# Expert slots of 512 tokens instead of 256, and the last batch finished inside the first slot

## The chip, the cores and the metric

The kernel runs on one core of one Trainium2 chip. The metric is the device time of one execution in microseconds (us). One execution of the kernel before was also taken with the hardware profiler; all rows below are of that execution, and times in them count from the start of its span.

## The reference

What is computed is hashed attention followed by a mixture of experts with one expert per token (all float32):

```
q, k, v: (4, 8, 768, 64)          proj: (64, 6)
bucket(z) = the 6 signs of z @ proj, read as a number
attn = softmax over keys in the query's bucket of 0.125 * q @ k^T   # else -1e9
x    = attn @ v, heads side by side            # (3072, 512)
logits = x @ w_gate + modality_bias[modality_id]      # 8 experts
e = argmax(logits);  g = softmax(logits)[e]
out[token] = g * (relu(x[token] @ w1[e]) @ w2[e])     # w1 512x1024, w2 1024x512
```

With the reference's inputs four of the eight experts get tokens: 1477, 1469, 98 and 28 of the 3072.

## The kernel before

There are two stages. The attention stage works on 16 pairs of heads (4 batches of 4 pairs; pair 15 is the last). Its TensorE order is written out by hand: the strings PLAN, one for each of six key steps (kt 0 to 5) of a pair, say in which order scores (S, lines 305 and 306), the weighted sums of values (A, line 341), the maxima of the next pair (M), the next pairs' preparation (T, B) and the finishing of an earlier batch follow each other. The softmax sums of a pair are added up by GpSimd, and for pair 15 half of them by VectorE (line 326, tile sp); sums(i), line 354, turns them into one row for each query with TensorE (line 361). finish(b), line 368, makes a batch's gate logits (lines 376 to 413) and calls route, line 593, which chooses the experts and scatters token numbers and gate weights into the table tab in DRAM (line 635). finish_x(b), line 417, turns a batch's x by TensorE (line 424), scales it on VectorE (line 426, tile xs, two buffers) and stores it to x_d in DRAM (line 428; from SyncE's queue, for the last batch from ScalarE's), in six tiles. Batch 2's six tiles are done in pairs 14 and 15, by the letters x and y of PLAN: in pair 15 tiles 3, 4 and 5 in the steps kt 2, 4 and 5. sums(15) is the last piece of the attention stage (line 518).

The expert stage (line 723) works in slots. A slot holds 256 tokens of one expert (TS, line 526; nt is 2) or, a small slot, 128. For a slot the token numbers come from tab by SyncE's queue (line 770), x is gathered by GpSimd's indirect DMA, 128 tokens at a time (line 774, tile xg), turned by TensorE (line 785) and split into a high and a low part by ScalarE and VectorE (lines 786 and 787, tiles xh and xl). The 4 MB of an expert's weights come in eight tiles of 512 KB (lines 752 and 754, tile raw, 4 buffers), and each is split in two parts (line 760 on ScalarE, line 762 on VectorE, for some of the first on GpSimd; tile w, 7 buffers). Tiles 0 to 3 of a slot are the first product (gemm1, line 790): two groups of 12 matmuls (lines 797 to 799) for each, whose result hps (PSUM, 3 buffers) is read by ScalarE (line 803) and then VectorE (line 804). Tiles 4 to 7 are the second product (gemm2, line 832, lines 839 to 841) into yps (PSUM, one bank per 128 tokens); store (line 843) scales by the gate weight and scatters to out (lines 846 and 847). Small slots go by gemm1_small and turn_small.

Each expert's tokens go to as many 256-slots as its count needs (a remainder up to 128 goes to a small slot). Two slots are early: they hold tokens of batches 0 to 2 alone, so that they don't wait for batch 3. After them come 10 sure slots and 2 sure small ones; further slots stand in conditional blocks behind them. In body (line 937) the order before is: the early slots' table (early_slots, line 685), x of the first slot, the first weights, all of finish(3), the tables of the late slots (late_slots, line 697), then slot 0 interleaved with finish_x(3), and the other slots. The slots in order are two early, eight late, a small one, two late, a small one.

In the expert stage the order on each engine is made by a scheduler from priorities in the order of the program and its own picture of time; every engine then runs its list in order. SBUF of the expert stage is that of the attention stage's tiles, given out from the bottom in the order of the pools.

Of the kernel before, what the change touches and what calls it, by code (L numbers as in the profile page):

```python
# [74 lines left out]
def attention(ctx, actx, tc, a, x_d, l_d, route=None, setup=None):  # L75
# [341 lines left out]
    def finish_x(b, lo, hi):  # L417
# [29 lines left out]
    with tc.manual_schedule(engines={mybir.EngineType.PE}):  # L447
# [19 lines left out]
        for i in range(NPR):  # L467
# [9 lines left out]
            for kt in range(NT):  # L477
                for c in PLAN[kt]:
# [39 lines left out]
        sums(NPR - 1)  # L518
# [7 lines left out]
TS = 256  # L526
DUMMY = E * N
EARLY = CFG["early"]
NBIG, SURE_BIG = 13, 12 - EARLY
NSML, SURE_SML = 8, 2  # L530


def host_consts_moe():
    def rep(x):
# [5 lines left out]
        "c_step": rep(np.stack([np.arange(12) * 256.0 + 255.5, np.arange(12) * 256.0 + 128.5])),  # L540
# [5 lines left out]
def router(ctx, tc, a, x_d, tab):  # L546
# [5 lines left out]
    step = const.tile([P, 2, 12], F32, name="kstep")  # L552
# [91 lines left out]
    def above(cnt, row, name):  # L644
        g = wk.tile([P, E, 12], F32, name="sg")
        nc.vector.tensor_tensor(out=g, in0=cnt.unsqueeze(2).broadcast_to([P, E, 12]), in1=step[:, row].unsqueeze(1).broadcast_to([P, E, 12]), op=ALU.is_gt)
# [76 lines left out]
def experts(ctx, tc, a, x_d, tab, out, ps_x, ident):  # L723
    nc = tc.nc
    w1, w2 = a["moe_w1"], a["moe_w2"]
    xp = ctx.enter_context(tc.tile_pool(name="xp", bufs=2))
    raw = ctx.enter_context(tc.tile_pool(name="raw", bufs=CFG["raw"]))
# [3 lines left out]
    hp = ctx.enter_context(tc.tile_pool(name="hp", bufs=10))  # L731
    ps_h = ctx.enter_context(tc.tile_pool(name="eps_h", bufs=3, space=PSUM))
    ps_y = ctx.enter_context(tc.tile_pool(name="eps_y", bufs=3, space=PSUM))
# [4 lines left out]

    def nt(s):
        return 1 if s[0] == "s" else 2  # L740
# [16 lines left out]
    def split(r, n):  # L757
        w = (wa if n % CFG["wp"] < 3 else wb).tile([P, 2, 1024], F32R, name="w")
        hi, lo = w[:, 0], w[:, 1]
        nc.scalar.copy(out=hi, in_=r)  # L760
        pool = n % 2 == 1 if n < CFG["pn"] else n % 8 in CFG["pm"]
        (nc.gpsimd if pool else nc.vector).tensor_tensor(out=lo, in0=r, in1=hi.bitcast(F32), op=ALU.subtract)  # L762
        return hi, lo

    def gather(s):
# [3 lines left out]
        tb = xp.tile([P, 2, 2], I32, name="tb", bufs=CFG["fd"] + 2)  # L769
        nc.sync.dma_start(out=tb[:, 0:n], in_=tab[bass.ds(o, n * P), :].rearrange("(p a) w -> p a w", a=n))  # L770
        xg = xp.tile([P, 2, DM], F32, name="xg", bufs=CFG["fd"] + 1)
        src = x_d[0:(B - 1) * S] if s[0] == "e" else x_d
        for g in range(n):
            nc.gpsimd.indirect_dma_start(out=xg[:, g], out_offset=None, in_=src, in_offset=bass.IndirectOffsetOnAxis(ap=tb[:, g, 0:1], axis=0))  # L774
        return tb, xg

    def xprep(s, xg):
        n = nt(s)
        xh = xp.tile([P, 4, TS], F32R, name="xh")
        xl = xp.tile([P, 4, TS], F32R, name="xl")  # L780
        for c in range(0, 4, 2):
            tp = ps_x.tile([P, 2, TS], F32, name="psx")
            for cc in range(2):
                for g in range(n):
                    nc.tensor.transpose(tp[:, cc, g * P:(g + 1) * P], xg[:, g, (c + cc) * P:(c + cc + 1) * P], ident)
            nc.scalar.copy(out=xh[:, c:c + 2, 0:n * P], in_=tp[:, :, 0:n * P])
            nc.vector.tensor_tensor(out=xl[:, c:c + 2, 0:n * P], in0=tp[:, :, 0:n * P], in1=xh[:, c:c + 2, 0:n * P].bitcast(F32), op=ALU.subtract)
        return xh, xl

    def gemm1(hi, lo, xh, xl, hh, hl):  # L790
        hi = hi.rearrange("p (c f) -> p c f", c=4)
        lo = lo.rearrange("p (c f) -> p c f", c=4)
        for fb in range(2):
# [8 lines left out]
            with tc.high_priority(offset=CFG["hpo"]):  # L802
                nc.scalar.activation(th, hps, AF.Relu)  # L803
                nc.vector.scalar_tensor_tensor(out=tl, in0=hps, scalar=0.0, in1=th.bitcast(F32), op0=ALU.max, op1=ALU.subtract)  # L804
# [3 lines left out]
    def gemm1_small(hi, lo, xh, xl):  # L808
        hi = hi.rearrange("p (c f) -> p c f", c=4)
        lo = lo.rearrange("p (c f) -> p c f", c=4)  # L810
        hps = ps_h.tile([P, TS], F32, name="hps")
# [4 lines left out]
        h = hp.tile([P, TS], F32, name="hn", bufs=2)  # L816
# [3 lines left out]
    def turn_small(h, hh, hl):  # L820
        tp = ps_h.tile([P, TS], F32, name="hps")
# [4 lines left out]
        nc.scalar.copy(out=th, in_=tp)  # L826
        nc.vector.tensor_tensor(out=tl, in0=tp, in1=th.bitcast(F32), op=ALU.subtract)  # L827
# [22 lines left out]
    class Runner:  # L850


        def __init__(self):
            self.raws, self.ws, self.got, self.xs = {}, {}, {}, {}
# [7 lines left out]
        def ahead(self):  # L862
            LS, LL = CFG["LS"], CFG["LL"]
            while True:
                did = False
                if self.nl < min(len(self.seq), self.n + LL + 1) and self.nl - self.ns < CFG["raw"]:
# [3 lines left out]
                elif self.ns < min(self.nl, self.n + LS + 1):  # L870
# [10 lines left out]
        def prepare(self, s):  # L881
            self.fetch(s)
            if s not in self.xs:
                self.xs[s] = xprep(s, self.got[s][1])

        def slot(self, k):
# [4 lines left out]
            for j in range(8):  # L891
                self.ahead()
                if j == CFG["fj"] and k > 0:
                    for s2 in self.order[k + 1:k + 1 + CFG["fd"]]:
                        self.fetch(s2)
                if j == 4:
                    yps = [ps_y.tile([P, DM], F32, name="yps") for _ in range(nt(s))]
                    if nxt:
                        self.prepare(nxt)
# [6 lines left out]
                elif nt(s) == 2:  # L906
# [27 lines left out]
    return Runner, tabs, conditional  # L934


def body(tc, a, out):
# [3 lines left out]
    with ExitStack() as ctx, ExitStack() as actx:  # L941
# [3 lines left out]
        runner, tabs, conditional = experts(ctx, tc, a, x_d, tab, out, ps_x, ident)  # L945
# [42 lines left out]
```

## Time and profile before

| | us |
|---|---|
| median of 3 runs | 866.99 |
| lowest, highest | 864.04, 867.5 |
| the profiled execution | 862.96 |
| its span | 861.1 |
| TensorE busy in the span | 801.3 |
| VectorE, ScalarE, GpSimd busy | 600.8, 498.3, 457.2 |
| mean granted TensorE clock | 0.977 of full speed |

The profiled execution lasted 862.96 us, of which 861.1 us are the span that the rows cover. Engines are PE (TensorE; PEld its weight loads), DVE (VectorE), ACT (ScalarE), POOL (GpSimd) and SP (SyncE, whose DMA queue is SPq). An arrow out<-in names the tile that is written and those that are read; xN is a count. A bracket at the end of a row gives the idle time of the engine before it and what ended that. Matmuls overlap in the pipeline, so that the time from one start to the next, and not a row's own length, is what one costs.

### The profile page before, as it was taken

How to read it: one execution, taken by the hardware profiler on the slowest of the kernel's cores; microseconds unless marked ns; L12 is line 12 of the kernel's file. 1: busy time of each engine (PE TensorE's matmuls, PEld its weight loads, DVE VectorE, ACT ScalarE, POOL GpSimd, SP SyncE). 2: the span in 40 equal slices, each digit the busy share in tenths (PEclk: the TensorE clock that was granted, in tenths of full speed). 3: DMA queues.
4: the chain of work that ended last, by engine and by line, in shares of the span. 5: the costliest groups of instructions: out<-in, count | busy, mean ns of one | idle time of the engine just before them, and what ended most of it. 6: DMA issues, size and time to landing. Idle time of an engine off the chain costs nothing.

```text
span 861.1 us, 14524 instructions
## 1 busy us (share of the span) xinstructions
PE 801.3 (93%) x5154; PEld 590.9 (69%) x5154; DVE 600.8 (70%) x1029; ACT 498.3 (58%) x953; POOL 457.2 (53%) x347
## 2 busy tenths in 40 slices
PE   6799999999999999999989787889999999999993
PEld 3466666666667656566746345779999999998992
DVE  6777678797877897776877767766555565567650
ACT  4567676676667566566744343355555555557551
POOL 5377779677887867976667664232222221122110
PEclk9899999999999999999999797999999999999997
DMA  6423212320431132132101254597777767679650
GB/s 173 112 75 92 74 43 68 93 74 19 118 116 63 55 93 74 56 99 68 38 19 31 72 160 147 113 325 222 222 218 232 222 214 234 200 230 299 215 148 22
DMA packets 76753, 110.87 MB, mean 129 GB/s; under 512 B 10495, under 2 KB 52095, under 8 KB 76672
## 3 DMA queue, kind: packets, MB, share of 16 engines
q1 hardware_dynamic: 70880, 95.14, 37.4%
q0 software_dynamic: 4928, 13.14, 4.1%
q10 hardware_dynamic: 864, 1.57, 0.6%
q8 instruction: 43, 0.70, 0.3%
q14 instruction: 38, 0.31, 0.2%
HBM read 84.83 MB, written 13.33 MB: 114 GB/s over the span
## 4 chain that ended last, share of the span: by engine, by line
PE 75%; DVE 10%; issue 6%; DMA 4%; ACT 2%; POOL 1%; SPq 1%; POOLq 0%; DVEq 0%; ACTq 0%
PE psu L341 13%; PE pss L305 8%; PE pss L306 7%; PE psm L239 5%; PE yps L839 5%; PE yps L841 5%; PE yps L840 5%; PE hps L797 4%; PE hps L799 4%; PE hps L798 4%; PE psx L207 3%; PE psx L180 3%; PE psm L245 3%; PE psx L222 2%; PE psx L268 1%
## 5 line engine op out<-in xcount | busy, mean ns | idle before, releaser
L326 POOL TENSOR_TENSOR sp<-sp,pb 128x768 f32<-128x768 f32 x124 | 224.9, 1849 | 38.3 <-ACT pb L323 38.1
L762 DVE TENSOR_TENSOR w<-raw,w 128x1024 fp32r<-128x1024 f32 x108 | 138.9, 1287 | 99.6 <-ACT w L760 93.7
L241 DVE TENSOR_REDUCE mx<-psm 128x1 f32<-128x512 f32 x192 | 131.3, 687 | 41.6 <-PE psm L239 40.4
L760 ACT CAST w<-raw 128x1024 fp32r<-128x1024 f32 x112 | 116.9, 1047 | 69.7 <-PE yps L841 50.7
L341 PE MATMUL psu<-pb,vt 128*64 128x512 f32 (+1 forms) x768 | 137.4, 501 | 0.0
L318 ACT ACTIVATE pb<-pss 128x512 f32<-128x512 f32 x192 | 112.9, 609 | 27.1 <-PE pss L306 18.6
L797 PE MATMUL hps<-xh,w 128*128 128x256 f32 x384 | 109.4, 286 | 2.1 <-DVE hl L804 1.9
L798 PE MATMUL hps<-xl,w 128*128 128x256 f32 x384 | 109.1, 284 | 0.0
L799 PE MATMUL hps<-xh,w 128*128 128x256 f32 x384 | 108.8, 284 | 0.0
L341 PEld LDWEIGHTS psu<-pb,vt 128*64 128x64 f32 x768 | 51.8, 139 | 79.8 <-issue 73.1
L774 POOL DMA_INDIRECT xg<-x_d,tb x26 | 32.7, 1259 | 123.6 <-DMA tb<-tab 115.7
L847 POOL DMA_INDIRECT out<-y,tb x26 | 33.9, 1305 | 117.2 <-ACT y L846 63.9
L839 PE MATMUL yps<-w,hl 128*128 128x512 f32 x208 | 82.9, 398 | 0.9 <-DVE hl L827 0.9
L841 PE MATMUL yps<-w,hh 128*128 128x512 f32 x208 | 81.3, 391 | 0.0
L840 PE MATMUL yps<-w,hh 128*128 128x512 f32 x208 | 81.0, 389 | 0.0
L323 ACT ACTIVATE pb<-pss 128x512 f32<-128x512 f32 x96 | 57.7, 601 | 38.5 <-PE pss L306 36.0
L305 PE MATMUL pss<-m_0g,s_0g 128*128 128x512 f32 x192 | 71.5, 372 | 6.3 <-DVE m_0g L270 3.9
L797 PEld LDWEIGHTS hps<-xh,w 128*128 128x128 f32 x384 | 73.9, 193 | 3.5 <-DVE hl L804 2.6
L798 PEld LDWEIGHTS hps<-xl,w 128*128 128x128 f32 x384 | 73.9, 192 | 1.2 <-issue 0.8
L799 PEld LDWEIGHTS hps<-xh,w 128*128 128x128 f32 x384 | 73.8, 192 | 0.0
L803 ACT ACTIVATE hh<-hps 128x256 fp32r<-128x256 f32 x96 | 36.6, 384 | 64.0 <-PE hps L799 57.9
L305 PE MATMUL pss<-m_1g,s_1g 128*128 128x512 f32 x192 | 69.5, 362 | 1.2 <-ACT pb L323 0.8
(214 smaller groups left out, 1773.3 us busy)
## 6 DMA issues: line engine op xcount, KB each, us to landing
raw<-moe_w SPq DMA_DIRECT2D x112, 512.0 KB
qk<-q SPq DMA_DIRECT2D x32, 192.0 KB
qk<-k SPq DMA_DIRECT2D x32, 192.0 KB
vt<-v SPq DMA_DIRECT2D x16, 384.0 KB
x_d<-xs SPq DMA_DIRECT2D x18, 256.0 KB
m_1g<-m_1g SPq DMA_DIRECT2D x16, 192.0 KB
s_1g<-s_1g SPq DMA_DIRECT2D x16, 192.0 KB
m_0g<-m_0g SPq DMA_DIRECT2D x15, 192.0 KB
```

The lines of the kernel that those rows point to most:

```text
L241: nc.vector.tensor_reduce(out=mx[:, qt + j, hi, 0:1], in_=mp, axis=AX.X, op=ALU.max)
L305: nc.tensor.matmul(out, t["s1"][h][:, ks], t["m1"][h][:, cs], start=True, stop=False)
L326: (nc.vector if h and i in CFG["spd"] else nc.gpsimd).tensor_tensor(out=t["sp"][:, h], in0=(t["pb"][0] if kt == 1 else t["sp"])[:, h], in1 ...
L341: nc.tensor.matmul(t["u"][part][64 * h:64 * h + 64, 0:w], t["v"][:, h, kt], t["pb"][kt][:, h, COLS[part]], start=False, stop=(kt == NT - 1 ...
L760: nc.scalar.copy(out=hi, in_=r)
L762: (nc.gpsimd if pool else nc.vector).tensor_tensor(out=lo, in0=r, in1=hi.bitcast(F32), op=ALU.subtract)
L797: nc.tensor.matmul(hps, lo[:, c, fs], xh[:, c], start=(c == 0), stop=False)
L798: nc.tensor.matmul(hps, hi[:, c, fs], xl[:, c], start=False, stop=False)
L799: nc.tensor.matmul(hps, hi[:, c, fs], xh[:, c], start=False, stop=(c == 3))
L839: nc.tensor.matmul(yps[g], hl[fc][:, gs], hi[:, fb], start=(fc == 0), stop=False)
L840: nc.tensor.matmul(yps[g], hh[fc][:, gs], lo[:, fb], start=False, stop=False)
L841: nc.tensor.matmul(yps[g], hh[fc][:, gs], hi[:, fb], start=False, stop=(fc == 7))
```

## The change

Slots hold 512 tokens (TS = 512): two early, four sure and two small ones, 8 slots in place of 14. gemm1's matmuls are 512 columns wide instead of 256, xprep turns four groups of tokens and is cut into halves that are done in the last two steps of the slot before. The pools change: two xg buffers of 512 tokens, one xh and xl, 5 buffers of w instead of 7, two of hps instead of three, four of yps instead of three, 8 of hh and hl. For early slots the token numbers are first limited to those of batches 0 to 2 by an operation on GpSimd (tile at). sums(15) moves from the end of the attention stage to the start of finish(3). All of finish(3) and finish_x(3) are interleaved with the eight steps of slot 0; the x tiles of batch 3 use the four buffers of y. In pair 15 tiles 3, 4 and 5 of batch 2's x are done ahead of the first score of kt 0, 1 and 2. late_slots and the late slots' tables follow slot 0.

```
@@ finish
+        if 4 * b + 4 == NPR:
+            sums(NPR - 1)
+            yield
@@ finish_x
-            xs = bp.tile([P, 512], F32, name="xs", bufs=2)
+            xs = pool.tile([P, 512], F32, name="y") if pool else bp.tile([P, 512], F32, name="xs", bufs=2)
@@ attention, the loop over pairs
             for kt in range(NT):
+                if i == NPR - 1 and kt < 3:
+                    next(xs, None)
+                    next(xs, None)
...
-        sums(NPR - 1)
@@ sizes
-TS = 256
+TS = 512
-NBIG, SURE_BIG = 13, 12 - EARLY
+NBIG, SURE_BIG = 11, 6 - EARLY
+RAW, WP, XG, LL = 4, 5, 2, 8
@@ experts
-    xp = ctx.enter_context(tc.tile_pool(name="xp", bufs=2))
+    gp = ctx.enter_context(tc.tile_pool(name="gp", bufs=1))
-    wa = ctx.enter_context(tc.tile_pool(name="wa", bufs=3))
-    wb = ctx.enter_context(tc.tile_pool(name="wb", bufs=CFG["wp"] - 3))
+    xp = ctx.enter_context(tc.tile_pool(name="xp", bufs=1))
+    wp = ctx.enter_context(tc.tile_pool(name="wp", bufs=WP))
+    hp = ctx.enter_context(tc.tile_pool(name="hp", bufs=8))
-    ps_h = ctx.enter_context(tc.tile_pool(name="eps_h", bufs=3, space=PSUM))
-    ps_y = ctx.enter_context(tc.tile_pool(name="eps_y", bufs=3, space=PSUM))
+    ps_h = ctx.enter_context(tc.tile_pool(name="eps_h", bufs=2, space=PSUM))
+    ps_y = ctx.enter_context(tc.tile_pool(name="eps_y", bufs=4, space=PSUM))
@@ gather
+            at = gp.tile([P, TS // P, 1], I32, name="at", bufs=2)
+            nc.gpsimd.tensor_scalar(out=at, in0=tb[:, :, 0:1], scalar1=(B - 1) * S - 1, scalar2=None, op0=ALU.min)
@@ slot
-                if j == CFG["fj"] and k > 0:
-                    for s2 in self.order[k + 1:k + 1 + CFG["fd"]]:
+                if j in (1, 4):
+                    for s2 in self.order[k + 1:k + 2 + j // 4]:
                         self.fetch(s2)
                 if j == 4:
                     yps = [ps_y.tile([P, DM], F32, name="yps") for _ in range(nt(s))]
-                    if nxt:
-                        self.prepare(nxt)
+                if j in (6, 7) and nxt:
+                    self.prepare(nxt, False)
@@ body
-            for _ in finish(B - 1):
-                pass
+        drive([(r.slot(0), 8, 0, 1), (chain(finish(B - 1), finish_x(B - 1, 0, NT, yp)), 26, 0.02, 1)])
         tabs["b"], tabs["s"], tot = late_slots()
...
-            drive([(r.slot(0), 8, 0, 1), (finish_x(B - 1, 0, NT), 12, 0, CFG["fxe"])])
```

## Rows read from the trace of the kernel before

**Rows 1.** The page's first part: busy time, share of the span and instructions of each engine.

```profile
PE 801.3 (93%) x5154; PEld 590.9 (69%) x5154; DVE 600.8 (70%) x1029; ACT 498.3 (58%) x953; POOL 457.2 (53%) x347
```

**Rows 2.** Stretches of time: the stretch in us from the span's start, its length, then busy us and instructions of PE, PEld, DVE, ACT and POOL, the granted PE clock, the DMA engines' busy share and GB/s. The first is the end of pair 14 and the start of pair 15, then the change from attention to experts, then about one full slot, and the end.

```profile
480.00:500.00 20.00, 13.71 (x64) 7.70 (x60) 12.38 (x10) 8.36 (x16) 9.66 (x6) 0.82 0.46 143
...
520.00:545.00 25.00, 19.40 (x144) 15.96 (x145) 21.59 (x50) 7.78 (x15) 10.96 (x8) 0.80 0.52 172
...
599.00:622.00 23.00, 23.00 (x152) 21.11 (x152) 13.74 (x19) 12.95 (x20) 5.37 (x4) 1.00 0.74 227
...
840.00:861.00 21.00, 7.36 (x40) 5.99 (x39) 1.27 (x3) 2.17 (x6) 1.19 (x2) 0.79 0.07 23
```

**Rows 3.** The same view over the whole expert stage up to its last matmul.

```profile
516.60:847.40 330.80, 317.94 (x2065) 285.68 (x2061) 206.88 (x318) 178.46 (x278) 78.75 (x60) 0.98 0.68 212
```

**Rows 4.** The chain that ended last, in two neighbouring full slots (start, us, what): the turns of x in one slot and in the next; the first and last of the 48 matmuls of a second product; the first and the last but one shown of a first product (84 matmuls from the one to the other, 83 steps).

```profile
599.93 0.87 PE psx L785 x8
623.23 0.87 PE psx L785 x8
...
624.10 0.23 PE yps L839
...
634.80 0.23 PE yps L841
635.03 0.12 PE hps L797
...
644.98 0.12 PE hps L799
```

**Rows 5.** The last small slot and the end of TensorE's work (the view of instructions in order of time: start, us, engine, line, operation): its first and its last matmul, then the last scatter.

```profile
835.04 0.28 PE L813 MATMUL hps<-w,xh 128*128 128x256 f32 x1
...
846.97 0.39 PE L841 MATMUL yps<-w,hh 128*128 128x512 f32 x1
...
848.36 0.98 POOL L847 DMA_INDIRECT out<-y,tb  x1 [8.15 <-ACT y L846]
```

**Rows 6.** Groups of instructions by line and form from 576 to 834 us: count, busy us, mean ns of one, and the idle time before them: the splitting of weights by VectorE and ScalarE, and the operations of both that read 512 columns out of PSUM.

```profile
L762 DVE TENSOR_TENSOR w<-raw,w 128x1024 fp32r<-128x1024 f32 x92 | 112.7, 1225 | 89.0 <-ACT w L760 87.5 <-PE hps L799 0.7 <-issue 0.5
L760 ACT CAST w<-raw 128x1024 fp32r<-128x1024 f32 x92 | 96.3, 1047 | 55.1 <-PE yps L841 49.9 <-DMA raw<-moe_w 3.1 <-issue 2.2
...
L787 DVE TENSOR_TENSOR xl<-psx,xh 128x512 fp32r<-128x512 f32 x20 | 12.8, 681 | 0.0
...
L786 ACT CAST xh<-psx 128x512 fp32r<-128x512 f32 x20 | 10.8, 595 | 0.5 <-PE psx L785 0.5
```

**Rows 7.** TensorE from the end of attention into the first slot, in order of time.

```profile
514.13 2.80 PE L341 MATMUL psu<-pb,vt 128*64 128x512 f32 x16
516.86 1.26 PE L361 MATMUL psx<-sp,ones 128*32 128x384 f32 x8
521.30 0.66 PE L785 MATMUL psx<-ident,xg 128*128 128x128 f32 x2 [3.19 <-DMA xg<-x_d,tb]
...
527.59 2.79 PE L376 MATMUL psx<-ut,gst 128*32 128x512 f32 x16 [2.38 <-DVE xl L787]
530.31 0.58 PE L798 MATMUL hps<-xl,w 128*128 128x256 f32 x1
```

**Rows 8.** The same view of the other engines there: the last three stores of batch 2's x on SyncE's queue, GpSimd's last addition of sums, its first gather for the first slot and its splitting of weights, and VectorE's splitting of weights.

```profile
504.45 10.82 SPq L428 DMA_DIRECT2D x_d<-xs  x3
...
514.60 1.82 POOL L326 TENSOR_TENSOR sp<-sp,pb 128x768 f32<-128x768 f32 x1 [1.81 <-ACT pb L323]
517.77 0.99 POOL L774 DMA_INDIRECT xg<-x_d,tb  x1 [1.35 <-DMA x_d<-xs]
...
520.04 4.67 POOL L762 TENSOR_TENSOR w<-raw,w 128x1024 fp32r<-128x1024 f32 x2
...
519.41 7.53 DVE L762 TENSOR_TENSOR w<-raw,w 128x1024 fp32r<-128x1024 f32 x2 [0.68 <-ACT w L760]
```

**Rows 9.** Pair 15's first steps on TensorE, in order of time: tile 2 of batch 2's x, the last of the four score matmuls that ran in kt 0 before the stall, the first behind it, the values' sums of kt 1, and the first score of kt 2.

```profile
481.64 0.63 PE L424 MATMUL psx<-ident,ut 128*128 128x128 f32 x4
...
483.83 0.40 PE L306 MATMUL pss<-m_1g,s_1g 128*128 128x512 f32 x1
488.10 0.55 PE L305 MATMUL pss<-m_0g,s_0g 128*128 128x256 f32 x1 [3.88 <-DVE m_0g L270]
...
490.57 4.40 PE L341 MATMUL psu<-pb,vt 128*64 128x512 f32 x16
...
498.22 0.50 PE L305 MATMUL pss<-m_0g,s_0g 128*128 128x512 f32 x1 [2.13 <-ACT pb L318]
```

**Rows 10.** VectorE and GpSimd over the same time: an operation on two elements a partition, for the early slots' table, the reader of a PSUM tile behind it, the scaling of tile 2, and GpSimd's additions of sums.

```profile
479.10 8.34 DVE L682 TENSOR_SCALAR selr<-selr 128x2 f32<-128x2 f32 x1
...
488.45 0.42 DVE L271 TENSOR_SCALAR lone<-psx 128x256 fp32r<-128x256 f32 x1
488.90 0.69 DVE L426 TENSOR_TENSOR xs<-psx,rin 128x512 f32<-128x512 f32 x1
...
473.22 14.19 POOL L326 TENSOR_TENSOR sp<-sp,pb 128x768 f32<-128x768 f32 x8
```

**Rows 11.** Whom TensorE waited for from 516 to 848 us: total us, times, the longest.

```profile
PE psx L785 <- DMA xg<-x_d,tb: 4.8, 4, 3.2
PE psx L376 <- DVE xl L787: 2.4, 1, 2.4
```

More of the change, by code (lines that the diff above doesn't have):

```diff
@@ L644, in above @@
     def above(cnt, row, name):
-        g = wk.tile([P, E, 12], F32, name="sg")
-        nc.vector.tensor_tensor(out=g, in0=cnt.unsqueeze(2).broadcast_to([P, E, 12]), in1=step[:, row].unsqueeze(1).broadcast_to([P, E, 12]), op=ALU.is_gt)
+        g = wk.tile([P, E, NSTEP], F32, name="sg")
+        nc.vector.tensor_tensor(out=g, in0=cnt.unsqueeze(2).broadcast_to([P, E, NSTEP]), in1=step[:, row].unsqueeze(1).broadcast_to([P, E, NSTEP]), op=ALU.is_gt)
         nb = wk.tile([P, E], F32, name=name)
@@ L775, in gather, with xprep @@
         return tb, xg
-    def xprep(s, xg):
-        n = nt(s)
+    def xprep(s, xg, dst):
         xh = xp.tile([P, 4, TS], F32R, name="xh")
         xl = xp.tile([P, 4, TS], F32R, name="xl")
[L781 to L788, printed above, removed]
+        dst += [xh, xl]
+        if nt(s) == 1:
+            tp = ps_x.tile([P, 4, P], F32, name="psx")
+            for c in range(4):
+                nc.tensor.transpose(tp[:, c], xg[:, 0, c * P:(c + 1) * P], ident)
+            nc.scalar.copy(out=xh[:, :, 0:P], in_=tp)
+            nc.vector.tensor_tensor(out=xl[:, :, 0:P], in0=tp, in1=xh[:, :, 0:P].bitcast(F32), op=ALU.subtract)
+            return
+        for c in range(4):
+            tp = ps_x.tile([P, TS], F32, name="psx")
+            for g in range(nt(s)):
+                nc.tensor.transpose(tp[:, g * P:(g + 1) * P], xg[:, g, c * P:(c + 1) * P], ident)
+            nc.scalar.copy(out=xh[:, c], in_=tp)
+            nc.vector.tensor_tensor(out=xl[:, c], in0=tp, in1=xh[:, c].bitcast(F32), op=ALU.subtract)
+            if c % 2:
+                yield
@@ L801, in gemm1 @@
             tl = hp.tile([P, TS], F32R, name="hl")
-            with tc.high_priority(offset=CFG["hpo"]):
-                nc.scalar.activation(th, hps, AF.Relu)
-                nc.vector.scalar_tensor_tensor(out=tl, in0=hps, scalar=0.0, in1=th.bitcast(F32), op0=ALU.max, op1=ALU.subtract)
+            nc.scalar.activation(th, hps, AF.Relu)
+            nc.vector.scalar_tensor_tensor(out=tl, in0=hps, scalar=0.0, in1=th.bitcast(F32), op0=ALU.max, op1=ALU.subtract)
             hh.append(th)
@@ L810, in gemm1_small @@
         lo = lo.rearrange("p (c f) -> p c f", c=4)
-        hps = ps_h.tile([P, TS], F32, name="hps")
+        hps = ps_h.tile([P, TS], F32, name="hps")[:, 0:256]
         for c in range(4):
@@ L820, in turn_small @@
     def turn_small(h, hh, hl):
-        tp = ps_h.tile([P, TS], F32, name="hps")
+        tp = ps_h.tile([P, TS], F32, name="hps")[:, 0:256]
         for fb in range(2):
@@ L825, in turn_small @@
         tl = hp.tile([P, TS], F32R, name="hl")
[L826 to L827 removed]
+        nc.scalar.copy(out=th[:, 0:256], in_=tp)
+        nc.vector.tensor_tensor(out=tl[:, 0:256], in0=tp, in1=th[:, 0:256].bitcast(F32), op=ALU.subtract)
         for fb in range(2):
@@ L968, in body @@
         r.extend(late)
-        if EARLY == 2:
-            drive([(r.slot(0), 8, 0, 1), (finish_x(B - 1, 0, NT), 12, 0, CFG["fxe"])])
-            k = 1
-        for k in range(k, len(r.order)):
+        for k in range(1, len(r.order)):
             drive([(r.slot(k), 8, 0, 1)])
```

67 lines of the change are left out of this document (31 added, 36 removed).

## The prediction

> **What bounds the kernel now.** I read the busy time first: TensorE works 801.3 us of a span of 861.1 us, no other engine above 70% [rows 1]. An average over two stages says little, so I went to stretches. In a full slot TensorE is busy 23.00 of 23 us at full clock with VectorE at 13.7 and ScalarE at 13.0 [rows 2]: a slot is bound by matmuls, and taking work from other engines there is worth nothing. The exceptions are pair 15's start (13.7 of 20 us busy, clock 0.82), the change from attention to experts (19.4 of 25, clock 0.80) and the end (7.4 of 21) [rows 2]. So there are two things to win: the price of the matmuls, and the holes between 480 and 545 us.
>
> The last sum of values starts at 514.13 and ends with the attention stage at about 516.6 [rows 7]; the last matmul of all ends at 847.4 [rows 5]. These 330.8 us hold 317.9 busy ones, so 12.9 idle [rows 3]. I count what they must hold. A slot's period is 23.30 us (623.23 less 599.93) [rows 4], so 12 slots are 279.6. The last small slot is 12.3 us from 835.04 to 847.4 [rows 5], with its four turns of x (half of 0.87 [rows 4]) 12.75, so two are 25.5. For batch 3's finish I estimate 6: six x tiles at no more than 0.63 [rows 9], the gate matmuls at half of 2.79, since they ran at half clock, and the sums at about 1 [rows 7]. Together 311; the other 19.7 us are lost: 12.9 idle, the rest clock and restarts. Behind the last matmul come 13.7 us of span (861.1 less 847.4), in which the last scatter is issued at 848.36 [rows 5] and nothing is changed.
>
> **512 columns in gemm1.** In one slot a 512-column matmul costs 10.70 / 47 = 0.2277 us, a 256-column one 9.95 / 83 = 0.1199 [rows 4]. Twelve slots of 96 narrow matmuls, 1152 x 0.1199 = 138.1 us, become 576 x 0.2277 = 131.2: 6.9 us less on the path. The second product has as many matmuls as before, and the turns of x too (16 x 0.109 for a large slot). A large slot is then 192 x 0.2277 + 1.74 = 45.5 us, six are 272.8 against 279.6.
>
> The rows give each narrow matmul a fixed cost of about 2 x 0.1199 - 0.2277 = 0.012 us over its columns. The Trainium skill (TensorE: Matmul & The Clock Gate, Part 1, "Wait — 56ns, not 53.3ns?") speaks against this gain: it puts a warm matmul's start-to-start at its columns by the clock and 2.5 ns more, by which 576 pairs would save an estimated 1.4 us. Here the rows' 12 ns decide.
>
> The 48 weight tiles that are no longer loaded take 48 x 1.05 us from ScalarE and 48 x 1.23 from VectorE [rows 6], and 24 MB of loads. All of it lies beside a TensorE that is full, so I cost it at nothing. If it weren't covered, it would only be a gain.
>
> **The first slot's start.** Now x is gathered from 517.77 on, once the third of the last three stores (issued from 504.45 to 515) has landed [rows 8]. Its first turns start at 521.30 after 3.2 us of waiting [rows 7]. Then VectorE takes 7.53 us for two splits of weights that cost 1.23 each elsewhere [rows 6, 8], because GpSimd splits two others at the same time (520.04 to 524.7), and x's low parts stand behind them. TensorE loses 2.4 us to that [rows 11] and works on at half clock; the first matmul that is followed by others without a hole is at 530.31 [rows 7]. After the change tiles 3 to 5 of x are turned at the start of kt 0, 1 and 2, and the last of them goes out at about 500 (kt 2 starts at 498.22 [rows 9]). Four gathers of about 1.3 us (twice two) then fit into the time in which TensorE finishes pair 15. x is there when attention ends, if SyncE's and GpSimd's lists put the stores and gathers there: the weight loads on SyncE and the sums and splits on GpSimd stand in the same lists. What then remains is the filling: four turns (0.44), ScalarE's copy (0.60) and VectorE's subtraction (0.68) [rows 6], 1.7 us, of which sums(15) covers some. I take 2 us idle and 2 for half clock behind it; before, the stretch to 530 cost over 10. Upper bound: the gathers come behind GpSimd's last sum as now (516.4), four take 5.1, the last lands 3.5 later (521.30 less 517.77), the filling makes 526.7, and the clock is low again: 13 us.
>
> **Pair 15.** Three turned tiles leave kt 2, 4 and 5 and enter kt 0, 1 and 2. Now TensorE stands from about 484 to 488.10, since VectorE is held for 8.34 us by an operation on two elements, which ends as GpSimd's run of sums ends (473.22 + 14.19 = 487.4) [rows 9, 10]. Tile 3 needs the PSUM buffer whose reader ends at 488.87 [rows 10]. So the four score matmuls that run before 484 now come behind it: they are queued behind the waiting turn, and ScalarE's exponentials wait for them. At half clock (16 value matmuls took 4.40 us there, 2.80 later [rows 9, 7]) that is 4 x 0.45 = 1.8 us more, and the two tiles in kt 0 and 1 come 1.7 us earlier in TensorE's list than they stood. Against it stands that TensorE later waits 2.13 us for an exponential behind a weight split [rows 9], which takes up some of the delay, and the 1.3 us that leave kt 2 to 5. I take +1, with +4 as the upper bound (1.8 + 1.7 and a wait for tile 3's scaling on VectorE, 0.7) and -8 as the lower: the table operation falls elsewhere, and the 3.9 us idle and some 3 of half clock go too.
>
> **Batch 3 inside slot 0, pools, late slots.** The finish's matmuls move between those of gemm1; there they wait for nothing long, since four to five of VectorE's short steps lie between them and 5.5 us of gemm1 cover each. Late tables and x are needed when slot 2 is prepared, over 80 us after slot 0 starts, so they cost nothing; without that cover the 1.2 us that TensorE waits for routing now would be the kind of price. The limit on early token numbers adds a short GpSimd operation per early slot, covered. Five w buffers hold 27 us of large slots; in small slots, 1.5 us a tile, five split and four raw tiles are more than the eight needed. With restarts as between mixed work now (2) and some waiting around the small slots (2, bounds 0 and 6), the lost time behind attention is 4 + 2 + 2 = 8 in place of 19.7.
>
> **The sum.** Against the profiled execution: -6.8 for columns, -11.7 for lost time, +1 for pair 15: -17.5, from 862.96 to 845.5. The median of the three runs lies 4.0 above that execution; taking the difference from it, I forecast 849.5, rounded to 849.
>
> **Rivals.**
> A. The stores or gathers do not get earlier, since they stand behind waiting entries of SyncE's or GpSimd's lists. For it: SyncE now puts three weight loads (which wait for splits) between the stores, and GpSimd's sums run until 516.4. Against: GpSimd's sums of pair 15 need only half its time. The start then costs 13 instead of 4: 858.
> B. VectorE's 8.34 us are not repeated, since the order of its list shifts. For it: the cause is a coincidence with GpSimd's additions. Against: everything ahead of that moment stays. Gain 9 more: 840.
> C. The evictions become the bound, the other side. With two hps buffers TensorE may come back to one after 12 x 0.2277 = 2.73 us; copying and subtracting 512 columns take 0.60 + 0.68 = 1.28 [rows 6], and with a weight split ahead on both engines (1.05 + 1.23) 3.56. So from 1.45 us of other work ahead it decides, and a group then costs 0.83: 48 groups cost 40 us, 889, slower by 2.5%; at one group in two it would be 869. For it: three buffers go to two. Against: in the order of the program a split stands behind the eviction that is already due, and VectorE is 40% idle. The Trainium skill (Perfetto Trace Analysis, "Optimization Strategy") names such repeated gaps as a sign of too few buffers; before the change no row shows one in a slot.
> D. The change does only half: x early, but waits of the scheduler's making in slot 0 (a turn or a gate matmul put where its input is late) keep 8 us of the holes: 857.
>
> **Chances.** The forecast 0.58, A 0.14, B 0.10, D 0.10, C 0.08 (half of that at its full price, the rest near 869). The range goes from B's 840 less the spread of 2 to A's 858 and 2 for its bounds: 838 to 860; C and a little beyond both ends are left out. A difference of about 0.5% (4.3 us) is what a measurement of this kernel can tell from no change. Faster 0.91, within 0.03, slower 0.06.
>
> **What would show it.** Six periods of about 45.5 us between preparations of x; no wait of TensorE for hl or hh in them (if there are, C). The last store of batch 2's x at about 500 and four gathers ahead of 516 (if behind, A). The first gemm1 matmul at 519 to 521. VectorE's operation for the early table at about 479 with several us (if not, B). In kt 0 of pair 15 the turn of tile 3 at about 489 and scores behind it. The last matmul at 827 to 832 and 13.7 us behind it. The forecast is wrong if the large slots take over 46.5 us or attention ends later than 521.

## The result and the profile after

The changed kernel takes 841.41 us (median of 4 runs, 840.04 to 842.87), the kernel before 867.25 (median of 4, 864.04 to 868.06): a ratio of 0.9709, 95% interval 0.9676 to 0.9742. The profiled execution of the changed kernel took 842.87 us with a span of 841.1. That is 20.1 us less than the profiled execution of before, while the medians are 25.8 apart: the profiled execution of before was 4.3 us below its median, that of after 1.5 above. Five more rounds on another chip gave 841.31 against 865.26, 24.0 apart (0.9736, 0.9700 to 0.9772).

The busy times of the page (to [rows 1]):

```profile
PE 791.5 (94%) x4578; PEld 560.1 (67%) x4578; DVE 538.2 (64%) x931; ACT 444.7 (53%) x855; POOL 449.2 (53%) x349
```

VectorE lost 63 us of work and ScalarE 54, and that is not why the kernel is faster: TensorE was the bound. The stretches of the changed kernel (columns as in [rows 2]): pair 15's start, the change to the expert stage, one stretch within the large slots, and, in the second fence, the whole expert stage.

```profile
480.00:500.00 20.00, 15.10 (x83) 9.68 (x83) 12.78 (x17) 7.51 (x16) 12.33 (x9) 0.91 0.46 147
...
514.00:545.00 31.00, 30.04 (x160) 21.09 (x157) 22.11 (x39) 14.89 (x22) 19.04 (x11) 1.00 0.49 154
...
600.00:645.00 45.00, 45.00 (x208) 37.43 (x207) 17.73 (x20) 17.30 (x24) 8.02 (x8) 1.00 0.46 140
```

```profile
518.10:827.40 309.30, 305.94 (x1481) 251.56 (x1479) 143.25 (x220) 125.50 (x180) 69.70 (x59) 1.00 0.50 146
```

The stretch around the change of stages, 19.4 of 25 us at clock 0.80 before [rows 2], is now 30.0 of 31 at full clock. TensorE there, in order of time (to [rows 7]), and its last matmul:

```profile
515.38 2.80 PE L341 MATMUL psu<-pb,vt 128*64 128x512 f32 x16
518.12 0.88 PE L803 MATMUL psx<-ident,xg 128*128 128x128 f32 x6
519.96 0.50 PE L816 MATMUL hps<-xh,w 128*128 128x512 f32 x1 [0.96 <-DVE w L769]
...
521.98 0.85 PE L361 MATMUL psx<-sp,ones 128*32 128x384 f32 x8
...
524.12 1.06 PE L379 MATMUL psx<-ut,gst 128*32 128x512 f32 x8
...
826.12 0.39 PE L859 MATMUL yps<-w,hh 128*128 128x512 f32 x1
```

Six of the first slot's 16 turns of x are done within pair 15, from 505.95 on, six more as soon as attention ends at 518.1, and the first product begins at 519.96, with one wait of 0.96 us. The sums and the gate matmuls lie between gemm1's. The expert stage lasts from 518.1 to 826.5, 308.4 us in place of the 330.8 that the prediction counted from about 516.6 [rows 3]: 22.4 less. Counted in both from the start of what follows the last value sums (516.86 before [rows 7]), it is 22.1 less. GpSimd and SyncE say why x was there (to [rows 8]): the last two stores are issued from 496.87 on, and the four gathers stand in the middle of pair 15's sums.

```profile
476.63 10.64 POOL L326 TENSOR_TENSOR sp<-sp,pb 128x768 f32<-128x768 f32 x6
...
502.32 1.07 POOL L785 DMA_INDIRECT xg<-x_d,at  x1 [1.69 <-issue]
503.70 0.96 POOL L785 DMA_INDIRECT xg<-x_d,at  x1 [0.30 <-issue]
504.97 1.57 POOL L785 DMA_INDIRECT xg<-x_d,at  x1 [0.30 <-ACT pb L323]
506.84 0.94 POOL L785 DMA_INDIRECT xg<-x_d,at  x1 [0.30 <-issue]
507.80 6.87 POOL L326 TENSOR_TENSOR sp<-sp,pb 128x768 f32<-128x768 f32 x3
```

```profile
496.87 2.66 SPq L431 DMA_DIRECT2D x_d<-xs  x2
```

Whom TensorE waited for from 514 to 830 us (to [rows 11], where the first two lines alone were 7.2 us):

```profile
PE hps L816 <- DVE w L769: 1.0, 1, 1.0
PE hps L816 <- ACT xh L804: 1.0, 1, 1.0
PE hps L816 <- DVE hl L822: 0.3, 1, 0.3
PE hps L831 <- ACT hn L835: 0.3, 1, 0.3
```

There is one wait of 0.3 us for an eviction (hl) in six large slots: two hps buffers are enough. In pair 15 (to [rows 9, 10]) time is still lost:

```profile
480.45 2.80 PE L341 MATMUL psu<-pb,vt 128*64 128x512 f32 x16
487.87 0.49 PE L268 MATMUL psx<-identr,nm 128*128 128x128 f32 x2 [4.62 <-ACT nm L258]
...
489.89 1.06 PE L427 MATMUL psx<-ident,ut 128*128 128x128 f32 x4
490.61 0.68 PE L305 MATMUL pss<-m_0g,s_0g 128*128 128x512 f32 x1
```

```profile
482.28 5.03 DVE L691 TENSOR_SCALAR selr<-selr 128x2 f32<-128x2 f32 x1
487.22 0.15 DVE L255 TENSOR_REDUCE m<-mx 128x4 f32<-128x8 f32 x1
```

The table's addition is held again (line 691 is line 682 of before), until 487.3, when GpSimd's run ends (476.63 + 10.64), and the pair's last maxima (line 255) stand behind it; tile 3 is turned at 489.89 and the scores stand behind it.

### The profile page after: what moved, and what is told of

Its sections match the earlier page's. It is cut to its first block, busy times and chain, and to the rows that moved or that the text cites. A ratio compares the mean times of both kernels' runs of the same rounds, so it can differ in the third digit from the quotient of the medians.

```text
span 841.1 us, 12853 instructions
## 1 busy us (share of the span) xinstructions
PE 791.5 (94%) x4578; PEld 560.1 (67%) x4578; DVE 538.2 (64%) x931; ACT 444.7 (53%) x855; POOL 449.2 (53%) x349
## 5 line engine op out<-in xcount | busy, mean ns | idle before, releaser
L769 DVE TENSOR_TENSOR w<-raw,w 128x1024 fp32r<-128x1024 f32 x60 | 76.6, 1277 | 96.9 <-ACT w L768 92.3
L865 POOL DMA_INDIRECT out<-y,tb x26 | 27.8, 1070 | 158.6 <-ACT y L864 93.5
L768 ACT CAST w<-raw 128x1024 fp32r<-128x1024 f32 x64 | 66.9, 1049 | 80.1 <-PE yps L859 72.9
L816 PE MATMUL hps<-xh,w 128*128 128x512 f32 x192 | 75.1, 393 | 2.2 <-DVE w L769 1.0
L817 PE MATMUL hps<-xl,w 128*128 128x512 f32 x192 | 74.9, 391 | 0.0
L818 PE MATMUL hps<-xh,w 128*128 128x512 f32 x192 | 74.5, 390 | 0.0
L247 DVE TENSOR_REDUCE mx<-psm 128x2 f32<-128x512 f32 x96 | 66.1, 689 | 6.9 <-PE psm L245 4.6
L821 ACT ACTIVATE hh<-hps 128x512 fp32r<-128x512 f32 x48 | 28.7, 598 | 79.1 <-PE hps L818 75.4
L305 PE MATMUL pss<-m_1g,s_1g 128*128 128x512 f32 x192 | 69.7, 363 | 0.7 <-ACT pb L323 0.3
L166 POOL TENSOR_TENSOR n<-qk,n 128x384 fp32r<-128x384 f32 x36 | 37.6, 1050 | 60.0 <-ACT n L162 51.2
L822 DVE SCALAR_TENSOR_TENSOR hl<-hps,hh 128x512 fp32r<-128x512 f32 x48 | 33.1, 689 | 53.9 <-ACT hh L821 52.3
L306 PE MATMUL pss<-m_1g,s_1g 128*128 128x512 f32 x192 | 65.5, 341 | 0.0
```

The costliest lines, as they stand in the source:

```text
L305: nc.tensor.matmul(out, t["s1"][h][:, ks], t["m1"][h][:, cs], start=True, stop=False)
L769: (nc.gpsimd if n < 8 and n % 2 else nc.vector).tensor_tensor(out=lo, in0=r, in1=hi.bitcast(F32), op=ALU.subtract)
L816: nc.tensor.matmul(hps, lo[:, c, fs], xh[:, c], start=(c == 0), stop=False)
L817: nc.tensor.matmul(hps, hi[:, c, fs], xl[:, c], start=False, stop=False)
L818: nc.tensor.matmul(hps, hi[:, c, fs], xh[:, c], start=False, stop=(c == 3))
```

## The experiments

All ratios are to the kernel before on the same chip in the same rounds. The runs were made on several chips, and the kernel before varies by 4 to 21 us from execution to execution within one set of rounds; where a few us matter I compare intervals within the traces as well. One is used throughout: pair 15 is measured from the start of pair 14's last value sums to that of its own (before 477.29 to 514.13, 36.8 us [rows 7]; after 480.45 to 515.38, 34.9). Each trace is of one execution, and the time ahead of pair 15 differs between traces, too; where that matters it is said.

**The changed kernel once more** (after_again).

> The changed kernel once more, five rounds beside the kernel before, so that parts can be compared on one chip. Theory: 841 us within 2, TensorE's expert stage at about 308 us from the end of attention to the last matmul. Rival (the difference of the medians is partly the spread of executions): the ratio to before comes nearer to 0.977, the ratio of the two profiled executions, than to 0.971.

841.31 us, 0.9736 (0.9700 to 0.9772); the last matmul ends at 824.4, 307.8 us after attention. The time is as expected, the ratio lies between the two expected ones: part of the 25.8 us is the spread of executions, and 24 is the better figure.

**The early x alone taken out** (x_late).

```
-                if i == NPR - 1 and kt < 3:
-                    next(xs, None)
-                    next(xs, None)
```

> The changed kernel with tiles 3 to 5 of batch 2's x back in kt 2, 4 and 5 of pair 15. Theory: the gathers come behind GpSimd's last sum again and x is first turned at 524 to 527, so 6 to 10 us slower than the changed kernel: 847 to 851. Rival 1 (the start is bound by the weight splits that wait for pair 15's space, not by x): within 2 us of it, 841 to 843. Rival 2 (the early tiles cost pair 15 as much as they bring): faster than it, 838 to 841.

853.92 us, 0.9898 (0.9861 to 0.9934): 12.6 us slower than after_again, more than expected. TensorE and GpSimd there:

```profile
511.14 2.80 PE L341 MATMUL psu<-pb,vt 128*64 128x512 f32 x16
522.22 0.66 PE L800 MATMUL psx<-ident,xg 128*128 128x128 f32 x2 [8.29 <-DMA xg<-x_d,at]
525.56 0.69 PE L800 MATMUL psx<-ident,xg 128*128 128x128 f32 x2 [2.68 <-DMA xg<-x_d,at]
526.90 1.36 PE L800 MATMUL psx<-ident,xg 128*128 128x128 f32 x4 [0.65 <-DMA xg<-x_d,at]
```

```profile
511.61 1.83 POOL L326 TENSOR_TENSOR sp<-sp,pb 128x768 f32<-128x768 f32 x1 [1.83 <-ACT pb L323]
513.42 3.03 POOL L766 TENSOR_TENSOR w<-raw,w 128x1024 fp32r<-128x1024 f32 x1
516.62 1.86 POOL L782 DMA_INDIRECT xg<-x_d,at  x1 [0.17 <-issue]
```

The gathers come behind the last sum and a weight split, and TensorE waits 11.6 us for them (8.29 + 2.68 + 0.65), in place of 3.9 for the two gathers of before's first slot (3.19 [rows 7] and 0.66), and the granted clock from 516 to 534 is 0.53. The expert stage, from 513.87 to 836.84, takes 323.0 us, 15.2 more than after_again's 307.8; pair 15 takes 32.9, 1.9 less. With 512 tokens a late x is dearer, and dearer than the 9 us between the prediction's bound of 13 and its 4. Both rivals fall.

**The finish ahead of slot 0** (finish_first).

```
-        if 4 * b + 4 == NPR:
-            sums(NPR - 1)
-            yield
+        sums(NPR - 1)          # at the end of attention, as before
-        drive([(r.slot(0), 8, 0, 1), (chain(finish(B - 1), finish_x(B - 1, 0, NT, yp)), 26, 0.02, 1)])
+        for _ in finish(B - 1):
+            pass
+        drive([(r.slot(0), 8, 0, 1), (finish_x(B - 1, 0, NT, yp), 12, 0, 1)])
```

> The changed kernel with sums(15) at the end of attention and all of finish(3) ahead of slot 0 in the program; only batch 3's x tiles stay inside slot 0. Theory (the interleaving removed the waits of TensorE for routing, 1.2 us, and for x behind attention's end): 2 to 5 us slower, 843 to 846, with TensorE idle ahead of the gate matmuls and the routing's. Rival (the scheduler fills these gaps from slot 0 by itself): within 1 us, 840 to 842.

845.75 us, 0.9786 (0.9751 to 0.9821): 4.4 us slower than after_again, as expected. TensorE's waits behind 505 us:

```profile
PE psx L801 <- DVE xl L803: 2.7, 2, 2.1
PE psx L620 <- DVE oh L615: 1.6, 1, 1.6
PE psx L361 <- POOL sp L326: 1.2, 1, 1.2
```

5.5 us in three places: for routing (oh), for GpSimd's last sum, which sums(15) now needs while nothing else may run, and behind x's low parts. Of the last, 2.1 us are at the start of slot 0 and 0.6 at 725.66, for a later slot. In the changed kernel's profiled execution none of the three lines is among the waits; in after_again's one is, 0.7 us for x's low parts at 720.82. So the interleaving removes 4.9 us of waits at the start.

**Neither of both** (slots_alone): both edits together.

> The changed kernel without both: x tiles in kt 2, 4 and 5 and finish(3) ahead of slot 0; what is left is the slots of 512 tokens with their pools. Theory: columns (6.8) and the waits between narrow slots (about 4) remain as the gain over before: 853 to 858. Rival (the larger slot hides the late start, since only one of the two edits is needed): 846 to 850. Rival (large slots alone are worth only the columns): 860.

857.82 us, 0.9928 (0.9907 to 0.9949): 7.4 us faster than before (865.26). That is the theory's upper edge, but not by its sum, as the trace below shows. With the other two runs this makes a square: early x is worth 12.1 us without the interleaving (857.82 to 845.75) and 12.6 with it (853.92 to 841.31); the interleaving 3.9 without early x and 4.4 with it. So these two add, within 0.5 us. (That 7.4, 12.1 and 4.4 make the 24.0 follows from the order in which they are taken and shows nothing more.) Pair 15 and TensorE's waits there:

```profile
477.58 4.49 PE L341 MATMUL psu<-pb,vt 128*64 128x512 f32 x16
...
510.26 2.80 PE L341 MATMUL psu<-pb,vt 128*64 128x512 f32 x16
```

```profile
PE psx L798 <- DMA xg<-x_d,at: 11.4, 3, 7.3
PE psx L617 <- DVE oh L612: 2.4, 1, 2.4
```

The expert stage (512.99 to 839.36) is 326.4 us, only 4.1 less than before's 330.5: the longer wait for gathers, 11.4 us in place of 3.9, takes up most of what the columns and the waits between narrow slots bring. Pair 15 gives another 4.2.

**The columns alone** (narrow).

```
-            for c in range(4):
-                nc.tensor.matmul(hps, lo[:, c, fs], xh[:, c], start=(c == 0), stop=False)
-                ...
+            for w in (slice(0, 256), slice(256, 512)):
+                for c in range(4):
+                    nc.tensor.matmul(hps[:, w], lo[:, c, fs], xh[:, c, w], start=(c == 0), stop=False)
+                    ...
```

> The changed kernel with each 512-column matmul of the first product cut into two of 256 columns on the same PSUM bank (576 more matmuls, the same columns, slots and buffers). Theory (a matmul costs 0.2277 us at 512 and 0.1199 at 256 columns, as in the rows of before): 6.9 us slower than the changed kernel, 848, and a large slot's period goes from 45.5 to 46.6 us. Rival (the fixed cost is the 2.5 ns that the Trainium skill states): 1.4 us slower, 843.

848.49 us, 0.9792 (0.9757 to 0.9826): 7.1 us above the changed kernel's 841.4, which was timed on another chip (the kernel before had 865.27 and 865.26 on the two). Two neighbouring turns of x, first of the changed kernel and then of this one:

```profile
606.36 1.04 PE L803 MATMUL psx<-ident,xg 128*128 128x128 f32 x8
...
651.69 1.03 PE L803 MATMUL psx<-ident,xg 128*128 128x128 f32 x8
```

```profile
607.18 1.04 PE L803 MATMUL psx<-ident,xg 128*128 128x128 f32 x8
...
653.82 1.03 PE L803 MATMUL psx<-ident,xg 128*128 128x128 f32 x8
```

The period is 45.33 us with 512 columns and 46.64 with 256: 1.31 for each large slot, or 13.6 ns for each of its 96 cut matmuls. The rows of before decide, not the 2.5 ns of the Trainium skill (TensorE: Matmul & The Clock Gate, Part 1, "Wait — 56ns, not 53.3ns?").

**Early x in the kernel before** (before_x_early): the three lines of x_late put into the kernel before.

> The kernel before with only tiles 3 to 5 of batch 2's x at the start of kt 0, 1 and 2 of pair 15. Theory (the early tiles free the first gathers whatever the slot's size; two gathers instead of four): 6 to 9 us faster than before, 856 to 859. Rival (there the first slot is held by the weight splits that VectorE and GpSimd do at once, 7.5 us, and finish(3) stands ahead of it anyway): 862 to 866. Rival 2 (GpSimd's or SyncE's list keeps the stores and gathers late): no change, 865.

861.14 us against 865.27, 0.9956 (0.9924 to 0.9987): 4.1 us, less than the theory's 6 to 9 and more than its rivals. TensorE in pair 15:

```profile
479.42 2.80 PE L341 MATMUL psu<-pb,vt 128*64 128x512 f32 x16
491.31 1.09 PE L424 MATMUL psx<-ident,ut 128*128 128x128 f32 x4 [7.87 <-DVE lone L271]
...
516.99 2.80 PE L341 MATMUL psu<-pb,vt 128*64 128x512 f32 x16
```

Here the prediction's price of pair 15 is seen: the four scores that ran ahead of the hold now stand behind the waiting turn, and TensorE waits 7.87 us instead of 3.88 [rows 9]. Pair 15 takes 37.6 us in place of 36.8. And only two gathers were late before: the expert stage (519.72 to 844.70) takes 325.0 us in place of 330.5.

This run and finish_first belong together, since both have the early x and finish(3) ahead of slot 0. Early x is worth 4.1 us with slots of 256 and 12.1 with slots of 512; the larger slots are worth 7.4 us with the late x and 15.4 (861.14 to 845.75) with the early one. So these two changes do not add: some 8 us of the gain come only when both are there, because the late x costs a large slot 11.4 us of waits (slots_alone) and a narrow one 3.9. The runs are on two chips whose times of before agree within 0.01 us; each difference has an uncertainty of 2 to 4 us.

**No weight split on GpSimd** (no_pool_split).

```
-        (nc.gpsimd if n < 8 and n % 2 else nc.vector).tensor_tensor(out=lo, ...)
+        nc.vector.tensor_tensor(out=lo, ...)
```

> The changed kernel with all weight splits on VectorE (the first eight tiles' odd ones were GpSimd's). Theory (VectorE and GpSimd slow each other when both split: 2.8 and 2.2 us for splits that cost 1.23 alone; TensorE waits 1 us for one of them): 1 to 2 us faster than the changed kernel, 839 to 840. Rival (VectorE's list at the start is the longer one then): 842 to 844.

841.20 us, 0.9713 (0.9683 to 0.9743), on another chip than after_again's 841.31: no difference that can be told. The wait for a split (1.0 us) is still there. Neither expectation holds: nothing is gained, and nothing is lost.

**No held addition** (no_hold_2).

```
-        nc.vector.tensor_reduce(out=r, in_=t, axis=AX.X, op=ALU.add)
-        nc.vector.tensor_scalar(out=r, in0=r, scalar1=float(DUMMY), scalar2=None, op0=ALU.add)
-        nc.vector.tensor_copy(out=out[:, 1], in_=r)
...
+        nc.vector.tensor_reduce(out=out[:, 1], in_=te, axis=AX.X, op=ALU.add)   # te: t and a ninth element, DUMMY
```

> The changed kernel with the slot tables' last steps done in one: the constant DUMMY stands as a ninth element in the row that is summed and the sum is written as an integer, so that the addition on VectorE that was held for 5.03 us while GpSimd added sums, and the conversion behind it, are gone. Theory (the hold costs pair 15 TensorE's 4.6 us of waiting and half clock behind it): 4 to 7 us faster than the changed kernel, 834 to 837. Rival 1 (pair 15 is bound elsewhere by then, by exponentials or GpSimd's sums): 840 to 842. Rival 2 (the next VectorE operation of that kind is held instead): 840 to 842 with a hold of several us at another line.

845.80 us, 0.9798 (0.9736 to 0.9861): not faster than the changed kernel's 0.9736, and the theory fell. The hold is gone, but pair 15 takes 37.8 us (478.95 to 516.74), 2.9 more than after_again's 34.9 (479.01 to 513.86). Neither rival foresaw why. VectorE's and TensorE's waits there:

```profile
DVE xs L429 <- DMA x_d<-xs: 9.2, 3, 4.9
```

```profile
PE psx L286 <- DVE xs L429: 3.0, 1, 3.0
...
PE psx L427 <- DVE xs L429: 1.7, 1, 1.7
```

With the table early, the first weight loads (2 MB) are issued from 483.34 on, among the stores of x, and three scalings of x tiles wait until an earlier tile has left one of the two xs buffers. Two stores issued among the loads landed after 4.4 and 5.8 us; the last two of pair 15, with no loads about them, after 2.0. The removed wait was covering another.

The execution has one more hold, far ahead of pair 15, that no trace of the changed kernel has:

```profile
246.30 7.07 DVE L166 TENSOR_TENSOR n<-qk,n 128x384 fp32r<-128x384 f32 x1
```

The same operation takes 0.56 us in the middle case, and at most 2.2 in after_again. TensorE waits 5.2 us behind it (to 254.03). The same hold, of 7.0 to 7.1 us, stands in the traces of before_no_hold and no_hold_no_pool, from the same chip, but not in sums_shared (same chip, addition kept) nor in no_hold_own_xs (same edit, another chip). Whether the edit or the chip brings it stays open, and the changed kernel itself was not run on that chip: the medians of these three runs are weak evidence against the edit. The stretch of pair 15 is the stronger one.

**The same edit in the kernel before** (before_no_hold).

> The kernel before with the same edit of the slot tables. Theory (its hold of 8.34 us costs TensorE 3.9 us idle, half clock behind it, and the table, so the first weights and x, come late): 5 to 9 us faster than before, 856 to 860. Rival (the late stores of x and the splits set the first slot's start anyway): 863 to 866.

863.97 us against 866.88, 1.0021 (0.9977 to 1.0064): the ratio says no change, though pair 15 is 3.2 us shorter (481.82 to 515.42, 33.6). Its first gather is issued at 519.06 as against 517.77 [rows 8]: there the late stores of x set the start, as the rival says. But pair 15 begins 4.5 us later in this execution, in part by the hold of 7.1 us at 248.5 that no_hold_2 has too, so that the 3.2 us do not reach the end. The 9 us that the prediction gave to rival B are not there.

**Both** (no_hold_no_pool): the edits of no_hold_2 and no_pool_split.

> The changed kernel with the table edit and all weight splits on VectorE. Theory (both add up, the second worth nothing by its own run): the same as the table edit alone within 1 us, 834 to 837. Rival (with pair 15 earlier the splits become the first slot's bound, and GpSimd's share then matters): 2 us or more away from it.

845.38 us, 0.9777 (0.9715 to 0.9839), as no_hold_2 within 1 us. The level that was expected is missed with it, the sum of the two is as expected.

**Pair 14's sums shared** (sums_shared): `spd=(15,)` becomes `spd=(14, 15)`.

> The changed kernel with half of pair 14's sums on VectorE as well (as pair 15's are), so that GpSimd's run of additions is shorter when the table's addition comes; the addition itself stays. Theory (it is held until GpSimd's run ends, whatever its own size): the hold is at most 2 us or absent, and the kernel 1 to 5 us faster than the changed one, less what VectorE's five more additions cost it: 837 to 841. Rival (the hold has another cause, such as a late input): still about 5 us; 841 to 845.

843.36 us, 0.9758 (0.9693 to 0.9823), with six executions from 835.54 to 844.85: inconclusive as a time. The hold is the point. VectorE, and the GpSimd run that was last ahead of it:

```profile
478.61 0.17 DVE L691 TENSOR_SCALAR selr<-selr 128x2 f32<-128x2 f32 x1
```

```profile
474.53 2.54 POOL L326 TENSOR_TENSOR sp<-sp,pb 128x768 f32<-128x768 f32 x1 [0.80 <-ACT pb L323]
```

GpSimd is idle from 477.07 on, and the same operation takes 0.17 us. So the hold comes from GpSimd's run and not from a late input. Pair 15 takes 33.2 us (475.87 to 509.05) in this trace, which is of the fastest of the six executions, 835.54 us.

**No hold, and own buffers for the x tiles** (no_hold_own_xs): no_hold_2 with

```
+            if b == B - 2 and tt >= 3:
+                xs = ld.tile([P, 2, NT, D], F32, name="qk").rearrange("p a t d -> p (a t d)")[:, 0:512]
```

> The run without the held addition, and with batch 2's x tiles 3 to 5 in three buffers of their own (the attention loads' tile qk, free by then) instead of the two of xs. Theory (without the hold, VectorE's scaling of tiles 2, 3 and 4 waited 9.2 us for earlier stores of x to land, TensorE 4.7 us for that, and half clock came behind it): these waits are gone, pair 15 from pair 14's last value sums to its own takes 31 to 33 us in place of 37.8, and the kernel 833 to 838, 0.961 to 0.967 of before. Rival (the scores of pair 15 are bound by exponentials and GpSimd's sums, so that it doesn't get under the changed kernel's 34.9): 840 to 844, 0.970 to 0.976 of before.

840.21 us, 0.9706 (0.9671 to 0.9742). Pair 15 is as the theory has it, 31.4 us:

```profile
479.62 2.80 PE L341 MATMUL psu<-pb,vt 128*64 128x512 f32 x16
...
504.93 0.45 PE L806 MATMUL psx<-ident,xg 128*128 128x128 f32 x1 [2.67 <-issue]
...
510.98 2.80 PE L341 MATMUL psu<-pb,vt 128*64 128x512 f32 x16
```

The waits for stores are gone, 6.4 us of pair 15 against no_hold_2. But the time falls into the rival's range. From that execution's trace, 3.5 us are gained in pair 15 on after_again and the last matmul ends at 822.1, 2.2 us before after_again's 824.4; the medians are 841.31 and 840.21 on two chips. The rest of the 3.5 us is spent outside: pair 15 begins 0.6 us later (479.62 against 479.01), and the expert stage takes 308.4 us against 307.8. So it is no faster version that the runs can tell from the changed kernel. The weight loads come behind the stores here (from 496.04 on), so the run does not separate the own buffers from the other order of the queue.

## Why the prediction was right, point by point

- The forecast was 849, measured 841.41: the right side, within the range, 8 us too high. It lies nearer to rival B's 840 than to the forecast, but not by B's mechanism: pair 15 gave 1.9 us in the profiled executions, where B's 9 us on top of the forecast's +1 would be 8.
- Columns: 6.9 us forecast; 7.1 by narrow's median and 1.31 x 6 = 7.9 by the slots' period. Right. The Trainium skill's figure (TensorE: Matmul & The Clock Gate, Part 1, "Wait — 56ns, not 53.3ns?") would have given an estimated 1.4; the runs disagree for these float32r matmuls.
- "A large slot is then ... 45.5 us": 45.33. Right, and the splits and loads that went away were worth nothing by themselves, as TensorE's 45.00 busy us of 45 show.
- The first slot's start, 4 us lost in place of over 10: the mechanism was right (stores at 497, gathers at 502 to 508 among GpSimd's sums, x turned at the end of attention). The size was off: TensorE is idle for 1 us there, and the 2 us of half clock never came, since the granted clock was 1.00 from 514 on. The other end was off too: x_late's expert stage is 15.2 us longer, where rival A's 13 less 4 gave 9. The upper bound counted the gathers and the filling; in x_late a weight split on GpSimd stands ahead of the gathers as well, and the clock is 0.53 from 516 to 534.
- "With restarts ... (2) and some waiting around the small slots (2) ... 8 in place of 19.7": of the 308.4 us, 45.33 x 6 + 25.5 + 6 = 303.5 are work, so 4.9 are lost. The forecast of 8 was too large by 3. Together with the columns this makes the 22.4 us of the expert stage, where 18.5 were forecast.
- Batch 3 inside slot 0: I put its worth into the lost time and did not price it alone; finish_first gives 4.4 us, with sums(15), routing and x's low parts as the waits that the interleaving removes.
- Pair 15, "+1": it became 1.9 us shorter in the profiled executions (36.8 to 34.9). The step that failed is that everything else in the pair stays. In slots_alone, without early x, it takes 32.7 us (477.58 to 510.26), so the larger slots shorten it by 4. The traces show two differences that can account for it, and no run separates them. No weight split is done inside it any more, and the wait of 2.13 us for an exponential behind one [rows 9] is gone. And the table's addition stands ahead of the maxima (line 255) in VectorE's list instead of behind them (before, the maxima are at 478.98 and the addition at 479.10), so that TensorE waits for the maxima, GpSimd gets no further work, and its run is of six additions and not of eight: the hold is 5.03 us and not 8.34. Early x costs 0.3 there (finish_first, 33.0). The first six turns of the slot's x, which in the changed kernel stand between the scores and wait 2.2 us for gathers, go with the other 2: with finish(3) ahead of slot 0 no turn stands in pair 15. The price that I feared is real only with the long hold (before_x_early, +0.7).
- The lower bound of pair 15, -8 by the hold's end: not so. Without the hold the stores of x take its place (no_hold_2, 37.8 us); with own buffers pair 15 takes 31.4, 5.4 less than before.
- The end: 14.6 us behind the last matmul, forecast 13.7.
- The sum on the profiled execution, -17.5, met -20.1. By the spans of the traces, -20.0, this is -22.1 for the expert stage, -1.9 for pair 15 and +0.8 behind the last matmul; and pair 15 began 3.2 us later than before (480.45 against 477.29), which no term of the sum has. In that execution the granted clock was 0.86 over the first 60 us and 0.97 from 420 to 470, against 0.91 and 1.00 before; the change touches nothing there, and in after_again the delay is 1.7, so I count it as spread. The remaining gap to 849 comes from the base: I took the difference from the median, 4 us above the execution that I read, and the changed kernel's profiled execution was 1.5 above its own.
- Rival A is what x_late shows, and didn't happen here. B happened in part: the order of VectorE's list did shift, and the hold fell from 8.34 to 5.03 us, but it stayed. "Everything ahead of that moment stays" was wrong. C did not happen: the single wait for hl is 0.3 us. D did not: no wait in slot 0 is over 1.0 us.

## What to carry to other kernels

Look for the first input of the next stage, and follow it back through every queue to the place where its production is put: moving three tiles 9 to 16 us earlier in a hand-written order was worth some 12 us here with slots of 512 tokens, and 4 with slots of 256. Two such changes need not add: larger slots make a late input dearer, so that each of the two was worth 8 us more with the other in place. Price them together. When a stage boundary is filled, put the serial chain (here routing) in pieces between the matmuls of the first independent work, so that each of its waits is covered. And before a stall is removed, ask what it was hiding: here the loads that came earlier met the stores that the next step waited for.

## What the runs showed of the hardware

An addition of VectorE on two elements, from SBUF to SBUF, waits until GpSimd's run of additions ends: 8.34 us to 487.4, when a run of eight ended [rows 10]; 5.03 us to 487.3, when one of six ended; 0.17 us with GpSimd idle (sums_shared). One of GpSimd's additions takes 1.77 us (14.19 by eight), so the waits are 4.7 and 2.8 of them. It is not for every operation: one of the same kind that reads 512 columns from PSUM (line 271) took 0.69 us at 480.95, within the same run of six. A subtraction with both inputs in SBUF, 0.56 us as a rule, was held for 7.07 us (no_hold_2). A reduction is not held. In the changed kernel, one pair earlier, one of them falls into a run of eight GpSimd additions; VectorE first, then GpSimd:

```profile
453.46 0.16 DVE L255 TENSOR_REDUCE m<-mx 128x4 f32<-128x8 f32 x1
```

```profile
445.54 14.39 POOL L326 TENSOR_TENSOR sp<-sp,pb 128x768 f32<-128x768 f32 x8 [8.77 <-ACT pb L323]
```

The Trainium skill (SBUF — State Buffer, "Who interferes with whom") says that VectorE and GpSimd share a pair of ports that one instruction holds for its whole length, that tensor_scalar can want it and that a reduction on this chip never does. The traces agree with the last two by the 5.03 and the 0.16 us above, and show in addition that the wait can go on over three to five GpSimd instructions in a row and not over one alone.
